# Later heads' scores as three fp32r products in the two halves of TensorE's rows, with three smaller edits to buffers and banks

## The chip, the cores and the metric

The kernel runs on one core of a Trainium2 chip. The core has TensorE (PE, with its weight loads shown apart as PEld), VectorE (DVE), ScalarE (ACT), GpSimd (POOL) and SyncE (SP), which here only issues DMAs. The metric is the device time of one execution in microseconds (us), lower is better. The kernel before takes 1144.28 us, the median of three runs (1142.51 to 1145.09).

## The reference, cut to what matters

Three pieces follow one another, all in fp32. The attention of 4 batches and 8 heads with 576 positions of 64 numbers keeps only the scores within tau of the row's largest; its output, 2304 tokens of 512 numbers, goes through an MLP with 2048 hidden numbers, and that one's through a second with two gates of 1536.

```python
scores = scale * np.matmul(q, k.transpose(0, 1, 3, 2))
thresh = np.max(scores, axis=-1, keepdims=True) - tau
scores = np.where(scores >= thresh, scores, -1000000000.0)
attn = np.exp(scores - np.max(scores, axis=-1, keepdims=True))
x = np.matmul(attn / (np.sum(attn, axis=-1, keepdims=True) + 1e-09), v)   # then heads side by side
h = x @ w_in;  x = (h * (1.0 / (1.0 + np.exp(-h)))) @ w_out               # MLP 1
out = ((x @ w_a) * (x @ w_b)) @ w_o2                                      # MLP 2
```

## The kernel before, in words

**Precision.** An fp32 matrix product is made of products of fp32r numbers: each operand is split into a high part (a cast to fp32r) and a low part (the rest, again fp32r), and high times high, low times high and high times low are summed in PSUM. Scores of the early heads, the transposes of the weighted scores (L577) and the products with v (L622) are plain fp32.

**Order.** All work is a list of tasks with an engine, a rank, an estimated cost and dependences. A planner (`Plan`) plays them through: each engine takes the ready task with the lowest rank. What comes out is a fixed order on each engine, and on the chip every engine works its list in that order. Ring sizes (`RINGS`) say how many buffers of a kind there are; a task that takes one waits for the one that many uses ago. A changed cost or ring can so reorder everything.

**Stages.** (1) Up to about 196 us: attention of batch 0 and part of batch 1, with scores in plain fp32 (L519), and beside it the 32 pieces of MLP 1's weights, loaded and split (`split_weight`). A 64-bit word of a weight is put together from two halves by ScalarE, VectorE (L354, L359) and an integer addition on GpSimd (`total`, L363, four pieces of 128 columns), then split (L367, L371). (2) 196 to 505 us: attention's later heads, with scores in fp32r (L512), mixed on TensorE with MLP 1's products of tokens in blocks of 256 (up L747, down L807). MLP 1's work has a higher rank and fills what attention leaves. (3) 505 to 718 us: MLP 1's last three blocks, of 256, 512 and 512 tokens, and the splitting of MLP 2's weights (`split_unit`), which are written to DRAM again. (4) From 718 us: MLP 2, three times 768 tokens, with seven products in place of eight; up products L1120, down products L1206.

**Scores.** A tile is 128 queries of one head by 576 keys. The keys stand in two halves of 288 (`NH`), one PSUM bank each, index j. For early heads (L519) q stands twice, in SBUF's partitions 0 to 63 and 64 to 127, and k's two halves stand one below the other, so that j = 0 uses the upper 64 rows of TensorE and j = 1 the lower 64. For later heads (from tile 54 on, `SPLIT_FROM`) the operand's 128 partitions hold q's high part above and q's low part below; k's high part stands twice, k's low part twice. One matmul over all 128 rows so gives high times k plus low times k. With k's high and low part and two halves that is four matmuls of 288 columns. Every fifth tile of a pair of heads has 64 queries of one head and 64 of the other: eight matmuls (four of them with 64 columns of weights).

**Closing attention.** Some buffers and PSUM banks of attention are given to MLP 1's last blocks when all of attention's tasks are done (`closed`), the stores of its output among them: the bank hc, the banks yc to yf, the buffers b5 of the 512-token blocks and those (`u`) in which MLP 2's weights are split.

**MLP 2's down products.** Each operand z is split by ScalarE (zh, L971) and VectorE (zl, L975) just before its 12 matmuls; there are two buffers of each. tm holds the sums between products, five buffers.

Of the kernel before, what the change touches and what calls it, by code (L numbers as in the profile page):

```python
# [21 lines left out]
P = 128  # L22
# [198 lines left out]
def pe_ns(n):  # L221
    return int(n * 0.4375 + 7)
# [3 lines left out]
def fused_kernel(ctx: ExitStack, tc: tile.TileContext, qk, qk2, v, tau, w_in, w_out, w_a, w_b, w_o2, out):  # L226
# [21 lines left out]
    def pool(stack, name, bufs, side="left", **kw):  # L248
# [3 lines left out]
    pools = {n: pool(ctx, n, size) for n, size in (("wy", N_YW), ("ws", N_SW), ("wz", N_TW))}  # L252
    p1, p1x, px, att, psb = (ExitStack() for _ in range(5))
    RINGS = dict(qk=2, sp=2, v=1, t=2, e=4, pa=1, pb=1, sa=1, sb=1, tp=2, hb=1, hc=1, yc=1, yd=1, ye=1, yf=1, xr5=2, x5=5, g5=2, th5=1, av=1, x=1, xi=1, rs=1,
                 xr=2, xb=8, g=2, th=1, yo=2, wraw=2, wc=1, wt=2, wy=N_YW, ws=N_SW, wz=N_TW,
                 ur=2, us=2, uw=2, vr=2, vs=2, vw=1, yr=1, pr=4, tm=5, a11=2, zh=2, zl=2, **{f"z{k}": 3 for k in range(5)})

# [17 lines left out]
    x_p = pool(att, "x", RINGS["x"])  # L275
    ps_s = pool(att, "ps_s", 1, space=PSUM)
    ps_t = pool(att, "ps_t", 2, space=PSUM)
    ps_av = pool(att, "ps_av", 1, space=PSUM)

# [48 lines left out]

    def split_weight(key, src, rank, dst, after=(), lo_engine="Pool", scale_engine="DVE", most=512):

# [64 lines left out]
    def w1_chunk(i, rank):  # L395
        dst = w_pool(i)
        j, i = divmod(i, 8)
        engines = dict(scale_engine=SCALE_ON[i % len(SCALE_ON)], lo_engine=LO_ON[i % len(LO_ON)], most=PIECE)
# [15 lines left out]
    def load_head(n, b, h, halves):  # L414
        s = {"split": False}
        cols = slice((0, 256)[halves[0]], (256 + NH, NH + S)[halves[-1]])

        def load():
            s["t"] = ap["qk"].tile([P, 2 * S], F32, name="qk")
            nc.sync.dma_start(out=s["t"][:, cols], in_=qk[b, h, :, cols])  # L420

        ld = dma(n + R_LD, P * 4 * (cols.stop - cols.start), load, take=["qk"])
        att_tasks.append(ld)
        s["ready"] = [ld]
        return s


    def split_head(n, b, h):
        s = {"split": True}

        def load():
            s["r"] = ap["qk"].tile([P, 2 * S], F32, name="qk")
# [6 lines left out]
        def lo_k():  # L439
            nc.vector.tensor_tensor(out=s["t"][:, 2], in0=s["r"][:, S:], in1=s["t"][:, 1].bitcast(F32), op=ALU.subtract)  # L440

        def lo_q(o):
            nc.gpsimd.tensor_tensor(out=s["t"][D:, 0, o], in0=s["r"][D:, o], in1=s["t"][D:, 0, o].bitcast(F32), op=ALU.subtract)

        ld = dma(n + R_LD, P * 8 * S, load, take=["qk"])
        up = add("ACT", act_ns(2 * S), n + R_SPLIT, hi, [ld], ["sp"], behind=closed0)
        qs = on_pool(S, n + R_SPLIT, lo_q, [up], PIECE)
        k = add("DVE", dve_ns(S), n + R_SPLIT, lo_k, [up], port=True)
# [45 lines left out]
    def softmax(parts, total):  # L494
# [203 lines left out]
    def load_x(j):  # L698
# [6 lines left out]
        def split(c):  # L705
# [11 lines left out]

            def lo(o):
                nc.gpsimd.tensor_tensor(out=s["l", c][:, o], in0=s["r", c][:, o], in1=s["h", c][:, o].bitcast(F32), op=ALU.subtract)  # L719
# [3 lines left out]
            l = on_pool(tn, R_AUX, lo, [h], PIECE)[-1]  # L723
            pl.free(raw, l)
# [5 lines left out]
    def mlp1_up(n, j, f):  # L730
# [54 lines left out]
    def mlp1_down(n, j, f):  # L785
# [27 lines left out]
        for k0 in (0, 4, 8):  # L813
            p = pl.add("PE", 4 * pe_ns(tn), R, down(k0), [g_ready[j, f][k0 == 8], *w_ready["out", f]],
                       banks if f == 0 and k0 == 0 else [], behind=[down_last[0], *([closed] if j >= 4 and f == 0 else [])])
            down_last[0] = p
# [446 lines left out]
    closed = pl.add("none", 1, 0, close_attention, behind=[*att_tasks, *closed0])  # L1263
    units = [(j, f) for j in range(len(BLOCKS)) for f in range(NF)]
# [83 lines left out]
```

## Time and profile before

| | before |
|---|---|
| median of 3 runs | 1144.28 us |
| the profiled execution's own time | 1144.45 us |
| its span | 1142.6 us |
| mean granted TensorE clock | 0.987 |
| PE busy | 1105.2 us (97%) |
| DVE busy | 822.8 us (72%) |
| ACT busy | 574.1 us (50%) |
| POOL busy | 201.9 us (18%) |
| chain that ended last | PE 81%, DMA 7%, DVE 5%, ACT 4% |

The span is what the trace covers; the execution's own time is 1.85 us more. Busy times of PE count a matmul from its start to the modelled end of its pipeline, so that neighbours overlap; the distance from one start to the next says more than the length of one. A plain fp32 matmul appears as two records. L with a number is a line of the kernel before.

### The profile page before, as it was taken

The numbers are of one execution on the slowest core, as the hardware profiler recorded it, in microseconds if no ns is written. First come the engines' busy times: TensorE is split into PE (matmuls) and PEld (weight loads), VectorE is DVE, ScalarE is ACT, GpSimd is POOL, SyncE is SP. The second block draws the span as 40 slices with busy tenths as digits, with TensorE's granted clock in tenths as the row PEclk, the third lists the DMA queues.
The fourth block names the chain that finished last, engine by engine and source line by source line (L and its number), as shares of the span: only waits on it lengthen the run. The fifth ranks groups of instructions, "written<-read, shape, count | busy, mean of one in ns | idle before, by whom it ended". The sixth has DMA issues, their size and how long they took to land.

```text
span 1142.6 us, 19524 instructions
## 1 busy us (share of the span) xinstructions
PE 1105.2 (97%) x7097; PEld 985.2 (86%) x7097; DVE 822.8 (72%) x1702; ACT 574.1 (50%) x1012; POOL 201.9 (18%) x386
## 2 busy tenths in 40 slices
PE   8889998999999999999999899999989999999998
PEld 6457766898889989999888688899989999999998
DVE  8888887777777777739888789566764668546664
ACT  7777776666766676646665645311332113411133
POOL 2445444333423343122000200000000000000000
PEclk9989999999999999999999899999999999999999
DMA  6554454222332232139999979988879878887882
GB/s 198 184 166 155 147 156 122 97 80 87 89 98 75 76 104 75 38 123 273 287 269 284 276 219 327 323 247 255 256 261 304 249 255 246 269 281 253 248 252 75
DMA packets 147231, 222.27 MB, mean 195 GB/s; under 512 B 8112, under 2 KB 107584, under 8 KB 147136
## 3 DMA queue, kind: packets, MB, share of 16 engines
q1 hardware_dynamic: 146992, 221.03, 62.4%
q8 instruction: 56, 0.92, 0.3%
q14 instruction: 39, 0.32, 0.1%
q10 hardware_dynamic: 144, 0.00, 0.0%
HBM read 173.74 MB, written 47.26 MB: 193 GB/s over the span
## 4 chain that ended last, share of the span: by engine, by line
PE 81%; DMA 7%; DVE 5%; ACT 4%; issue 2%; POOL 1%; SPq 0%; POOLq 0%; DVEq 0%; ACTq 0%
PE pr L1120 23%; PE hb L747 11%; PE pr L1206 9%; PE sb L807 8%; PE av L622 6%; PE tp L577 5%; PE hc L747 5%; PE sa L512 4%; PE yc L807 2%; PE yd L807 2%; PE ye L807 2%; PE yf L807 2%; DMA wraw<-w_out 1%; DMA xi<-r_d 1%; DMA wraw<-w_in 1%
## 5 line engine op out<-in xcount | busy, mean ns | idle before, releaser
L1120 PE MATMUL pr<-w 128*128 128x384 f32 x1512 | 262.6, 334 | 0.0
L1120 PEld LDWEIGHTS pr<-w 128*128 128x128 f32 x1512 | 262.2, 188 | 0.1
L747 PE MATMUL hb<-xh,w 128*128 128x256 f32 (+1 forms) x704 | 156.9, 312 | 2.6 <-DVE th L760 1.9
L528 DVE TENSOR_SCALAR_CACHE_REDUCE t<-sa,nscale 128x576 f32<-128x576 f32 x128 | 103.5, 809 | 53.0 <-PE sa L512 45.5
L1206 PE MATMUL pr<-zh,w 128*128 128x384 f32 x504 | 129.2, 338 | 0.0
L545 DVE SCALAR_TENSOR_TENSOR e<-t,thr,e 128x576 f32<-128x576 f32 x128 | 112.0, 876 | 23.8 <-ACT e L542 22.3
L747 PEld LDWEIGHTS hb<-xh,w 128*128 128x128 f32 x704 | 113.9, 191 | 12.8 <-DVE th L760 3.1
L577 PE MATMUL tp<-ident,e 128*128 128x128 f32 x706 | 107.5, 280 | 12.0 <-DVE e L545 7.5
L577 PEld LDWEIGHTS tp<-ident,e 128*128 128x128 f32 x706 | 79.7, 142 | 36.4 <-issue 14.2
L542 ACT ACTIVATE e<-t,min 128x576 f32<-128x576 f32 x128 | 99.8, 781 | 19.7 <-DVE t L528 18.7
L747 PE MATMUL hb<-xl,w 128*128 128x256 f32 (+1 forms) x352 | 107.1, 304 | 0.7 <-POOL xl L719 0.7
L807 PE MATMUL sb<-gh,w 128*128 128x256 f32 (+1 forms) x576 | 98.1, 301 | 0.0
L1206 PEld LDWEIGHTS pr<-zh,w 128*128 128x128 f32 x504 | 91.9, 190 | 0.0
L1206 PE MATMUL pr<-zl,w 128*128 128x384 f32 x252 | 86.4, 343 | 4.9 <-DVE zl L975 4.8
L807 PEld LDWEIGHTS sb<-gh,w 128*128 128x128 f32 x576 | 80.1, 190 | 6.3 <-issue 3.3
L971 ACT CAST zh<-z 128x768 fp32r<-128x768 f32 x45 | 37.5, 833 | 84.1 <-PE pr L1206 58.4
L363 POOL TENSOR_TENSOR wt<-wc,wt 128x128 uint32<-128x128 uint32 x128 | 62.3, 517 | 77.3 <-DVE wc L359 48.4
L1132 ACT COPY yo<-pr 128x384 f32<-128x384 f32 x18 | 8.7, 481 | 123.7 <-PE pr L1120 123.7
L747 PEld LDWEIGHTS hb<-xl,w 128*128 128x128 f32 x352 | 67.1, 191 | 3.7 <-POOL xl L719 0.9
L512 PE MATMUL sa<-sp 128*128 128x288 f32 (+1 forms) x400 | 69.9, 300 | 0.0
L584 ACT COPY pb<-tp 128x512 f32<-128x512 f32 (+2 forms) x128 | 60.3, 493 | 17.7 <-PE tp L577 17.5
L719 POOL TENSOR_TENSOR xl<-xr,xh 128x128 fp32r<-128x128 f32 x72 | 39.3, 574 | 165.5 <-ACT xh L716 160.9
(140 smaller groups left out, 2016.6 us busy)
## 6 DMA issues: line engine op xcount, KB each, us to landing
w<-wab_d SPq DMA_DIRECT2D x126, 512.0 KB
w<-wo_d SPq DMA_DIRECT2D x63, 512.0 KB
wab_d<-uw SPq DMA_DIRECT2D x18, 896.0 KB
qk<-qk SPq DMA_DIRECT2D x20, 576.0 KB
wo_d<-uw SPq DMA_DIRECT2D x10, 896.0 KB
wraw<-w_in SPq DMA_DIRECT2D x16, 512.0 KB
wraw<-w_out SPq DMA_DIRECT2D x16, 512.0 KB
v<-v SPq DMA_DIRECT2D x20, 320.0 KB
```

What stands on the lines that cost most here:

```text
L363: nc.gpsimd.tensor_tensor(out=s["t"][:, o], in0=s["c"][:, o].bitcast(U32), in1=s["t"][:, o], op=ALU.add)
L512: nc.tensor.matmul(s["s"][:r + m, j, :NH], lhsT=hd["t"][:, 0, c - r:c + m], rhs=hd["t"][:, k, j * NH:(j + 1) * NH], start=(k == 1), stop=( ...
L528: nc.vector.tensor_scalar(out=s["t"], in0=s["s"][:, :, :NH], scalar1=nscale, scalar2=None, op0=ALU.mult, op1=ALU.min, accum_out=s["min"])
L542: nc.scalar.activation(out=s["e"], in_=s["t"], func=AF.Exp, scale=-1.0, bias=s["min"])
L545: nc.vector.scalar_tensor_tensor(out=s["e"], in0=s["s"][:, :, :NH] if early else s["t"], scalar=s["thr"], in1=s["e"], op0=ALU.is_ge if ear ...
L577: nc.tensor.transpose(t["tp"][:, j * P:(j + 1) * P], e["e"][:, o:o + P], ident)
L584: nc.scalar.copy(out=dst(s["p"]), in_=t["tp"][:, :m * P] if m < 4 else t["tp"].rearrange("p (k q) -> p k q", k=4))
L622: nc.tensor.matmul(s["av"][h * D:(h + 1) * D, :nq], lhsT=v["v"][:, h, k], rhs=s["p"][:, k, h * nq:(h + 1) * nq], start=(k == 0), stop=(k = ...
L747: nc.tensor.matmul(s["h"], lhsT=w[:, a, o:o + P], rhs=xx, start=(c == 0 and k == 0), stop=(c == NC - 1 and k == 2))
L807: nc.tensor.matmul(ys[j][e // per][:, e % per * tn:(e % per + 1) * tn], lhsT=w[:, a, e * P:(e + 1) * P], rhs=gs[j, f][g], start=(f == 0 an ...
L1120: nc.tensor.matmul(bank[:, m, :TN], lhsT=w["w"][:, a, (2 * m + k) * P:(2 * m + k + 1) * P], rhs=y[i][x][:, k, :TN], start=(i in (1, 6, 5) ...
L1206: nc.tensor.matmul(bank[:, c, :TN], lhsT=w["w"][:, a, (2 * e + c) * P:(2 * e + c + 1) * P], rhs=z[x][:, e], start=(i in (1, 6, 5) and sl = ...
```

## The change

- Later heads: q's and k's high parts stand in one operand, the low parts in another, both laid out as for early heads. Three products (high high, low high, high low) are made for each half of the keys, j = 0 in rows 0 to 63 and j = 1 in rows 64 to 127: six matmuls of 288 columns and 64 rows in place of four of 128 rows. What is loaded and split is 864 columns in place of 1152. The planner's cost of a tile is three matmuls in place of four.
- zh has three buffers in place of two, tm four in place of five.
- Attention's PSUM pools stand in a stack of their own, closed when attention's tasks on PE, ACT and DVE are done (`closed_p`). Only hc and the yc to yf banks wait for that; the buffers wait for `closed` as before.
- The integer addition of the weights' third and fourth quarter (j above 1) moves from GpSimd to VectorE, and so does the low part of the last token block's x.
- The planner's costs for MLP 2's weight preparation are lower.

```diff
-                 ..., tm=5, a11=2, zh=2, zl=2, ...
+                 ..., tm=4, a11=2, zh=3, zl=2, ...
...
-    ps_s = pool(att, "ps_s", 1, space=PSUM)
+    ps_s = pool(attp, "ps_s", 1, space=PSUM)
...
         def total(o):
-            nc.gpsimd.tensor_tensor(out=s["t"][:, o], in0=s["c"][:, o].bitcast(U32), in1=s["t"][:, o], op=ALU.add)
+            eng = nc.gpsimd if total_engine == "Pool" else nc.vector
+            eng.tensor_tensor(out=s["t"][:, o], in0=s["c"][:, o].bitcast(U32), in1=s["t"][:, o], op=ALU.add)
...
+        ..., total_engine=("Pool", "DVE")[j > 1])
...
         def hi():
-            s["t"] = pools["sp"].tile([P, 3, S], F32R, name="sp")
-            nc.scalar.copy(out=s["t"][:, :2], in_=s["r"].rearrange("p (a s) -> p a s", a=2))
+            s["t"] = pools["sp"].tile([P, 2, S + NH], F32R, name="sp")
+            nc.scalar.copy(out=s["t"][:, 0], in_=s["r"])
...
+        def lo(eng, o):
+            eng.tensor_tensor(out=s["t"][:, 1, o], in0=s["r"][:, o], in1=s["t"][:, 0, o].bitcast(F32), op=ALU.subtract)
...
                 for hd, c, r, m in reversed(parts):
-                    for j in range(2):
-                        for k in (1, 2):
-                            nc.tensor.matmul(s["s"][:r + m, j, :NH], lhsT=hd["t"][:, 0, c - r:c + m], rhs=hd["t"][:, k, j * NH:(j + 1) * NH],
-                                             start=(k == 1), stop=(k == 2), skip_group_check=True)
+                    for k, (a, x) in enumerate(((0, 0), (1, 0), (0, 1))):
+                        for j in range(2):
+                            rows = slice(j * D, (j + 1) * D)
+                            nc.tensor.matmul(s["s"][:r + m, j, :NH], lhsT=hd["t"][rows, a, c - r:c + m], rhs=hd["t"][rows, x, S:],
+                                             start=(k == 0), stop=(k == 2), skip_group_check=True)
...
-        cost = 4 * pe_ns(NH) * len(parts) if parts[0][0]["split"] else 780
+        cost = 3 * pe_ns(NH) * len(parts) if parts[0][0]["split"] else 780
...
+            if j == len(BLOCKS) - 1:
+                l = pl.add("DVE", dve_ns(tn), R_AUX, lambda: lo(slice(0, tn), nc.vector), [h], port=True)
...
-                       behind=[up_last[0], *([closed] if c == 0 and bank == "hc" else [])])
+                       behind=[up_last[0], *([closed_p] if c == 0 and bank == "hc" else [])])
...
+    def close_banks():
+        attp.close()
         pools["hc"] = pool(p1, "ps_hc", 1, space=PSUM)
         pools["y5"] = pool(p1, "ps_y5", 1, space=PSUM)
...
+    closed_p = pl.add("none", 1, 0, close_banks, behind=[t for t in att_tasks if t["engine"] in ("PE", "ACT", "DVE")])
```

What it moves, at three places. First, TensorE at the first mixed tile of the later heads; L512 and L514 are the scores, L577 and L579 transposes, L622 and L624 products with v, L747, L752, L807 and L812 MLP 1. Before:

```order
L577 MATMUL tp<-ident,e 128x128 x6
L512 MATMUL sa<-sp 128x288 x4
L627 MATMUL av<-ident,sums 128x128
L807 MATMUL sb<-gh,w 128x256 x4
L807 MATMUL sb<-gl,w 128x256 x4
L622 MATMUL av<-pa,v 64x256 x10
L577 MATMUL tp<-ident,e 128x128 x4
L512 MATMUL sa<-sp 128x288 x4
L512 MATMUL sa<-sp 64x288 x4
L577 MATMUL tp<-ident,e 128x128 x6
```

And of the changed kernel, at its first mixed tile:

```order
L812 MATMUL sb<-gh,w 128x256 x4
L514 MATMUL sa<-sp 128x288 x6
L812 MATMUL sb<-gh,w 128x256 x4
L579 MATMUL tp<-ident,e 128x128 x6
L812 MATMUL sb<-gl,w 128x256 x4
L629 MATMUL av<-ident,sums 128x128
L624 MATMUL av<-pa,v 64x256 x10
L579 MATMUL tp<-ident,e 128x128 x4
L514 MATMUL sa<-sp 128x288 x6
L514 MATMUL sa<-sp 64x288 x6
L579 MATMUL tp<-ident,e 128x128 x6
```

A tile's scores stand alone between other matmuls, as before: there are 90 such places in either order, and no two tiles' scores follow one another.

Second, ScalarE where the 512-token block before the last ends: yo copies the sums out of PSUM (L827, L832), th and gh belong to the next block's first units, us, vs, uw and vw to MLP 2's weights. Before:

```order
L827 ACTIVATE yo<-ye 128x512
L827 ACTIVATE yo<-sb 128x512
L898 CAST vw<-vs 128x896
L757 ACTIVATE th_8561<-hb 128x512
L870 ACTIVATE vs<-vr 128x512
L873 ACTIVATE vs<-vr 128x512
L763 CAST gh_8562<-th_8561 128x512
```

And of the changed kernel:

```order
L832 ACTIVATE yo<-ye 128x512
L875 ACTIVATE us<-ur 128x512
L878 ACTIVATE us<-ur 128x512
L762 ACTIVATE th_8730<-hb 128x512
L903 CAST vw<-vs 128x896
L768 CAST gh_8731<-th_8730 128x512
L832 ACTIVATE yo<-sb 128x512
```

The copy out of sb stood ahead of the next block's th and gh and now stands behind them; a pair us that needs a loaded weight stands ahead of th.

Third, SyncE in MLP 2's first down products: w are the streamed weights, yr the next 768 tokens' input. Before:

```order
L960 DMA w<-wab_d 128x1024 x30
L960 DMA w<-wo_d 128x1024 x15
L995 DMA yr<-yT_d 128x2x768
L960 DMA w<-wo_d 128x1024
L995 DMA yr<-yT_d 128x2x768
L960 DMA w<-wo_d 128x1024 x5
```

And of the changed kernel:

```order
L965 DMA w<-wab_d 128x1024 x30
L965 DMA w<-wo_d 128x1024 x13
L1000 DMA yr<-yT_d 128x2x768
L965 DMA w<-wo_d 128x1024 x2
L1000 DMA yr<-yT_d 128x2x768
L965 DMA w<-wo_d 128x1024 x6
```

The two loads of yr are issued two and one weight loads earlier.

## Rows read from the trace of the kernel before

**Rows 1.** The page's first line.
```profile
span 1142.6 us, 19524 instructions
```

**Rows 2.** Four stretches: busy of PE, PEld, DVE, ACT, POOL; granted clock, DMA share, GB/s.
```profile
0.00:196.00 196.00, 173.92 (x1193) 122.96 (x1193) 159.48 (x417) 145.70 (x279) 83.34 (x173) 0.96 0.53 161
196.00:505.00 309.00, 307.93 (x2491) 276.43 (x2491) 223.03 (x623) 201.02 (x391) 101.51 (x186) 1.00 0.27 83
505.00:718.00 213.00, 208.05 (x1071) 177.23 (x1070) 180.89 (x349) 129.13 (x213) 17.06 (x29) 0.98 0.92 276
718.00:1142.00 424.00, 415.27 (x2347) 408.54 (x2345) 259.40 (x315) 98.23 (x130) 0.00 (x0) 0.99 0.79 250
```

**Rows 3.** Later heads' scores by form: count, busy us, mean ns, idle before.
```profile
L512 PE MATMUL sa<-sp 128*128 128x288 f32 x360 | 64.6, 301 | 0.0
...
L512 PE MATMUL sa<-sp 128*64 128x288 f32 x40 | 6.9, 294 | 0.0
```

**Rows 4.** PE in time, one later tile: start, length, instruction.
```profile
301.31 0.69 PE L512 MATMUL sa<-sp 128*128 128x288 f32 x4
...
301.84 0.64 PE L807 MATMUL sb<-gl,w 128*128 128x256 f32 x4
```

**Rows 5.** PE and PEld in time, an early tile between MLP 1's matmuls.
```profile
104.07 0.64 PE L807 MATMUL sb<-gh,w 128*128 128x256 f32 x4
104.64 0.76 PE L519 MATMUL sa<-qk 64*128 64x288 f32 x4
105.32 0.74 PE L807 MATMUL sb<-gh,w 128*128 128x256 f32 x4
105.90 0.28 PE L807 MATMUL sb<-gl,w 128*128 128x256 f32 x1
...
105.32 0.54 PEld L807 LDWEIGHTS sb<-gh,w 128*128 128x128 f32 x4 [0.39 <-issue]
```

**Rows 6.** PE in time, the first two tiles, right behind plain fp32 matmuls.
```profile
4.29 0.50 PE L287 MATMUL av<-sums 128*128 128x128 f32 x3
4.72 0.76 PE L519 MATMUL sa<-qk 64*128 64x288 f32 x4
5.31 0.65 PE L519 MATMUL sb<-qk 64*128 64x288 f32 x4
5.89 0.33 PE L575 MATMUL tp<-ident 128*128 128x128 f32 x1
```

**Rows 7.** PE in time, a later mixed tile, its last four with 64 columns.
```profile
309.96 1.29 PE L512 MATMUL sa<-sp 128*128 128x288 f32 x8
311.09 0.27 PE L577 MATMUL tp<-ident,e 128*128 128x128 f32 x1
```

**Rows 8.** ACT and PE in time where the next-to-last block of MLP 1 ends.
```profile
646.30 0.60 ACT L827 ACTIVATE yo<-sb 128x512 f32<-128x512 f32 x1 [3.17 <-DMA yT_d<-yo]
...
647.63 0.60 ACT L757 ACTIVATE th<-hb 128x512 f32<-128x512 f32 x1
...
651.00 1.22 PE L807 MATMUL yc<-gh,w 128*128 128x512 f32 x2 [4.30 <-ACT gh L763]
```

**Rows 9.** Two stretches, columns as in Rows 2.
```profile
640.00:660.00 20.00, 15.70 (x58) 12.33 (x57) 14.80 (x30) 10.91 (x18) 2.03 (x4) 0.83 0.96 289
840.00:860.00 20.00, 17.53 (x94) 17.21 (x93) 12.00 (x13) 5.89 (x8) 0.00 (x0) 0.91 0.74 251
```

**Rows 10.** PE and DVE in time, down products of MLP 2.
```profile
833.20 0.44 PE L1206 MATMUL pr<-zl,w 128*128 128x384 f32 x1 [0.78 <-DVE zl L975]
...
841.39 0.96 DVE L1007 TENSOR_TENSOR yt<-yr 128x768 f32<-128x768 f32 x1 [2.25 <-DMA yr<-yT_d]
...
844.27 0.69 PE L1206 MATMUL pr<-zl,w 128*128 128x384 f32 x1 [2.47 <-DVE zl L975]
```

**Rows 11.** Groups: the integer addition on DVE (MLP 2's) and POOL.
```profile
L887 DVE CUSTOM_DVE_ANT_0 us<-us 128x1024 uint16<-128x1024 uint16 x28 | 19.2, 684 | 0.0
...
L363 POOL TENSOR_TENSOR wt<-wc,wt 128x128 uint32<-128x128 uint32 x128 | 62.3, 517 | 77.3 <-DVE wc L359 48.4 <-DVE thr L536 18.5 <-DVE sums L477 5.9
```

More of the change, by code (lines that the diff above doesn't have):

```diff
@@ L252, in fused_kernel @@
     pools = {n: pool(ctx, n, size) for n, size in (("wy", N_YW), ("ws", N_SW), ("wz", N_TW))}
-    p1, p1x, px, att, psb = (ExitStack() for _ in range(5))
+    p1, p1x, px, att, attp, psb = (ExitStack() for _ in range(6))
     RINGS = dict(qk=2, sp=2, v=1, t=2, e=4, pa=1, pb=1, sa=1, sb=1, tp=2, hb=1, hc=1, yc=1, yd=1, ye=1, yf=1, xr5=2, x5=5, g5=2, th5=1, av=1, x=1, xi=1, rs=1,
                  xr=2, xb=8, g=2, th=1, yo=2, wraw=2, wc=1, wt=2, wy=N_YW, ws=N_SW, wz=N_TW,
-                 ur=2, us=2, uw=2, vr=2, vs=2, vw=1, yr=1, pr=4, tm=5, a11=2, zh=2, zl=2, **{f"z{k}": 3 for k in range(5)})
+                 ur=2, us=2, uw=2, vr=2, vs=2, vw=1, yr=1, pr=4, tm=4, a11=2, zh=3, zl=2, **{f"z{k}": 3 for k in range(5)})
     right = ctx.enter_context(ExitStack())
@@ L275, in fused_kernel @@
     x_p = pool(att, "x", RINGS["x"])
-    ps_s = pool(att, "ps_s", 1, space=PSUM)
-    ps_t = pool(att, "ps_t", 2, space=PSUM)
-    ps_av = pool(att, "ps_av", 1, space=PSUM)
+    ps_s = pool(attp, "ps_s", 1, space=PSUM)
+    ps_t = pool(attp, "ps_t", 2, space=PSUM)
+    ps_av = pool(attp, "ps_av", 1, space=PSUM)
     sums = const.tile([P, P], F32, name="sums")
@@ L327, in fused_kernel, with split_weight @@
     wt, w_ready = {}, {}
-    def split_weight(key, src, rank, dst, after=(), lo_engine="Pool", scale_engine="DVE", most=512):
+    def split_weight(key, src, rank, dst, after=(), lo_engine="Pool", scale_engine="DVE", most=512, total_engine="Pool"):
         s = {}
@@ L379, in split_weight @@
         j = pl.add("DVE", dve_ns(512), rank, join, [h, c], port=True)
-        ts = on_pool(512, rank, total, [j, l], most)
+        if total_engine == "Pool":
+            ts = on_pool(512, rank, total, [j, l], most)
+        else:
+            ts = [pl.add("DVE", dve_ns(512), rank, lambda: total(slice(0, 512)), [j, l], port=True)]
         pl.free("wc", ts[-1])
@@ L397, in w1_chunk @@
         j, i = divmod(i, 8)
-        engines = dict(scale_engine=SCALE_ON[i % len(SCALE_ON)], lo_engine=LO_ON[i % len(LO_ON)], most=PIECE)
+        engines = dict(scale_engine=SCALE_ON[i % len(SCALE_ON)], lo_engine=LO_ON[i % len(LO_ON)], most=PIECE, total_engine=("Pool", "DVE")[j > 1])
         if i < 4:
@@ L418, in load @@
         def load():
-            s["t"] = ap["qk"].tile([P, 2 * S], F32, name="qk")
+            s["t"] = ap["qk"].tile([P, S + NH], F32, name="qk")
             nc.sync.dma_start(out=s["t"][:, cols], in_=qk[b, h, :, cols])
@@ L431, in load @@
         def load():
-            s["r"] = ap["qk"].tile([P, 2 * S], F32, name="qk")
+            s["r"] = ap["qk"].tile([P, S + NH], F32, name="qk")
             nc.sync.dma_start(out=s["r"], in_=qk2[b, h])
         def hi():
-            s["t"] = pools["sp"].tile([P, 3, S], F32R, name="sp")
-            nc.scalar.copy(out=s["t"][:, :2], in_=s["r"].rearrange("p (a s) -> p a s", a=2))
[L439 to L448, printed above, removed]
+            s["t"] = pools["sp"].tile([P, 2, S + NH], F32R, name="sp")
+            nc.scalar.copy(out=s["t"][:, 0], in_=s["r"])
+        def lo(eng, o):
+            eng.tensor_tensor(out=s["t"][:, 1, o], in0=s["r"][:, o], in1=s["t"][:, 0, o].bitcast(F32), op=ALU.subtract)
+        ld = dma(n + R_LD, P * 4 * (S + NH), load, take=["qk"])
+        up = add("ACT", act_ns(S + NH), n + R_SPLIT, hi, [ld], ["sp"], behind=closed0)
+        qs = on_pool(S, n + R_SPLIT, lambda o: lo(nc.gpsimd, o), [up], PIECE)
+        k = add("DVE", dve_ns(NH), n + R_SPLIT, lambda: lo(nc.vector, slice(S, S + NH)), [up], port=True)
         att_tasks.extend([ld, *qs])
@@ L716, in hi, with lo @@
                 nc.scalar.copy(out=s["h", c], in_=s["r", c])
-            def lo(o):
-                nc.gpsimd.tensor_tensor(out=s["l", c][:, o], in0=s["r", c][:, o], in1=s["h", c][:, o].bitcast(F32), op=ALU.subtract)
+            def lo(o, eng=nc.gpsimd):
+                eng.tensor_tensor(out=s["l", c][:, o], in0=s["r", c][:, o], in1=s["h", c][:, o].bitcast(F32), op=ALU.subtract)
             ld = dma(-1, P * 4 * tn, load, after=need, take=[raw], slack=SLACK, behind=[closed] if big else [])
             h = pl.add("ACT", act_ns(tn), R_AUX, hi, [ld], [ring])
-            l = on_pool(tn, R_AUX, lo, [h], PIECE)[-1]
+            if j == len(BLOCKS) - 1:
+                l = pl.add("DVE", dve_ns(tn), R_AUX, lambda: lo(slice(0, tn), nc.vector), [h], port=True)
+            else:
+                l = on_pool(tn, R_AUX, lo, [h], PIECE)[-1]
             pl.free(raw, l)
@@ L814, in mlp1_down @@
             p = pl.add("PE", 4 * pe_ns(tn), R, down(k0), [g_ready[j, f][k0 == 8], *w_ready["out", f]],
-                       banks if f == 0 and k0 == 0 else [], behind=[down_last[0], *([closed] if j >= 4 and f == 0 else [])])
+                       banks if f == 0 and k0 == 0 else [], behind=[down_last[0], *([closed_p] if j >= 4 and f == 0 else [])])
             down_last[0] = p
@@ L849, in dv @@
     def dv(n):
-        return int(n / 0.96 + 170)
+        return int(n / 0.96 + 67)
     def ac(n):
-        return int(n / 1.2 + 180)
+        return int(n / 1.2 + 93)
     stored = {}
```

5 lines of the change are left out of this document (2 added, 3 removed).

## The prediction

> **What bounds the kernel now.** I read the span [rows 1], then the table of busy times by stage [rows 2]. From 196 to 505 us, where the later heads' scores stand, PE is busy 307.93 of 309 us at full clock; VectorE 223, ScalarE 201, and DMA's share is 0.27. The reader is to see that whatever TensorE gains or loses there is gained or lost by the whole, and that edits on other engines in that stage (a shorter cast, a shorter VectorE subtraction, a smaller load) are worth nothing. Before 196 us PE lacks 22 us and VectorE is busy 159 of 196: neither is full. From 505 to 718 and from 718 on PE is full again but for a few single waits, found by reading PE's timeline for gaps [rows 8, 10].
>
> **The scores.** Before: 360 + 40 matmuls [rows 3], four to a part, so 100 parts, of which ten pairs make mixed tiles: 90 separate places on PE. One tile of four takes 301.84 - 301.31 = 0.53 us, 0.13 us a matmul [rows 4], and loses nothing at its ends. Together 400 x 0.13 = 52 us.
>
> After: 600 matmuls over half the rows. Whether two of them run side by side, the early heads show: their matmuls use 64 rows in the same alternation. And they show what it costs to go into the halves and out again. In [rows 5] four matmuls of MLP 1 take 0.64 us to the last's end and one alone 0.28, so they start 0.12 us apart. From 104.07 to 105.90 us there are eight of them, 0.96 us; the tile between takes 1.83 - 0.96 = 0.87 us. How much of this is streaming? Two tiles on end take 5.89 - 4.72 = 1.17 us to the next instruction [rows 6], one takes 105.32 - 104.64 = 0.68 [rows 5]: the second tile costs 0.49 us. It has four records of 288 columns. Plain fp32 over all rows takes 0.11 us for one of 128 columns (three in 0.50 us less the 0.27 of one alone [rows 6, 7], halved), so 0.25 for 288, and four in a row 1.0 us: the halves do run side by side. The remaining 0.87 - 0.49 = 0.38 us are lost at the two changes: TensorE starts 104.64 - 104.07 - 4 x 0.12 = 0.09 us late, then waits for its first weights; behind the tile the next weight load starts only after 0.39 us without one, in which nothing is named as awaited [rows 5], where otherwise weights are loaded under the matmul before.
>
> Is that the halves' doing or plain fp32's? In [rows 6] plain fp32 matmuls over all 128 rows stand ahead of the first tile: three from 4.29 us on, at 0.11 us, should let the next start at 4.62 and it starts at 4.72. The number type doesn't change there, the rows do. Against this stands [rows 7]: 128 columns of weights to 64, in fp32r, costs nothing (eight in 1.13 us). So a change of columns alone is free in fp32r; a change of rows in fp32r no row shows. I take the 0.38 us for each place.
>
> The Trainium skill has rules for both sides. Its page "TensorEngine Tiling (Array Packing)", section Key Properties, says that a change of the tiling mode drains the engine; that agrees with [rows 5, 6] and speaks against this change, though [rows 7] shows a change of columns without one; it states no price, so the sum goes by the rows. "TensorE: Matmul & The Clock Gate", Part 3, lets tiles in different rows run at the same time, some 4 ns apart, and by that alone the change would save a quarter of the scores' time; [rows 6] agrees with the concurrency.
>
> After, then: 100 parts x 3 x 0.13 = 39 us, 13 less than before; 90 x 0.38 = 34 us more; within a mixed tile a change from 128 to 64 columns of weights in halved rows, ten times 0 [rows 7] to 0.38 us, I take 1 us. **Sum +22 us.** Its ends: -13 (nothing lost at the changes) and, with halves one after another, 600 x 0.13 - 52 + 34 = +60.
>
> **The third zh.** PE waits for zl 0.78 us at 833 us, as long again at the same place of the next 768 tokens, and 2.47 us at 844 [rows 10]. The first two are the cast that waits for one of two zh; with three, two casts stand ahead of the copy of the sums. The long one is VectorE, which sits 2.25 us at L1007 until yr has landed, with the zl behind it; yr's loads now stand one and two weight loads earlier, and a product of 12 matmuls (each such load feeds one) lasts about 2 us, so it should land in time. The clock was 0.91 from 840 to 860 us [rows 9]: 20 x 0.09 x 2 = 3.6 us at 1.2 GHz instead of 2.4, in part the wait itself, so about 1 us lost. Together 0.78 + 0.78 + 2.47 + 1 = **-5 us**; ends 0 and -6. The missing fifth tm would show as PE waiting for a copy behind the output's stores; no wait of this kind is near, I give it 0.
>
> **The last-but-one block's end.** PE waits 4.30 us for gh; ScalarE stood 3.17 us before the copy of sb, waiting for a store of yo to land, and th and gh were queued behind it [rows 8]. The clock is 0.83 there [rows 9], 6.8 us at the lower level, about 2 us lost beyond the wait. In the new order th and gh go first, but a pair us, which needs a loaded weight while DMA's share is 0.92 [rows 2], stands ahead of them. **-4 us**; ends -6.5 and +3 (the same wait at another place).
>
> **The first stage.** Sixteen integer additions go to VectorE: the same operation for MLP 2's weights takes 0.684 us [rows 11], 16 x 0.684 = 11 us on an engine with 36 us free; 64 pieces of 0.517 us leave GpSimd. A weight's chain gets shorter by 4 x 0.517 - 0.684 = 1.4 us, the weights are split before tile 45 instead of 54 in VectorE's order, and 474 instead of 408 matmuls of MLP 1 stand ahead of the first later score, 66 x 0.12 = 8 us of work for PE's 22 idle us. So +11 to -8; I take **0**.
>
> **Banks, and the later close.** The order leaves 66 instead of 159 matmuls of MLP 1 between the last score and the first use of hc: attention ends 11 us nearer to it. The banks' own wait is covered by 66 x 0.12 = 8 us. What still waits for `closed` starts that much later against PE: the 512-token blocks' loads, covered by the 256-token block's 16 units of 24 matmuls, 46 us; and MLP 2's weights, where DMA's share is 0.92 [rows 2] and SyncE's and ScalarE's queues are held up with it. I take 0; if that cover is gone it costs up to 11 us. The last block's x on VectorE: 0, four operations where it has 32 us free.
>
> **Sum.** 22 - 5 - 4 = +13. The profiled execution took 1144.45 us (span 1142.6 and 1.85 around it), 0.2 above the median of the runs. 1144.45 + 13 = **1158 us**.
>
> **Rivals.**
> - *The change of rows is free in fp32r*, as that of columns is [rows 7]. Then the scores save 13 us, and with the other gains 1144.45 - 13 - 9 = 1122: faster than before. For it: no row shows fp32r in halves; against it: [rows 6]. It decides where a place costs below (13 + 9) / 90 = 0.24 us; there the change is even. By the Trainium skill's Part 3 named above this would be the outcome.
> - *Half the price*: the wait for the rows to empty, but weights loaded ahead. 90 x 0.19 = 17: +17 - 13 - 9, about 1140.
> - *fp32r halves take turns*, though fp32's don't, so that the change doesn't do what it says: 600 x 0.13 = 78 us, 1158 + 39 = 1197.
>
> **How the numbers follow.** The forecast has 0.74, its own range 1146 to 1172 (-12: first stage and ends of the waits' terms; +14: late weights or waits that stay). Free rows 0.16, half the price 0.05, turns 0.05. 0.2% of the time, 2.3 us, is about what can be told from no change. Faster: 0.16 + 0.03 + 0.01 of the forecast's tail = 0.20. Same 0.05. Slower 0.75. To leave out no more than 2 in 10 the range reaches into the free rows' case: 1120 to 1173.
>
> **What would show it.** PE's timeline around the new scores: a tile of six should take about 0.8 us between its neighbours' rhythm, with a stretch without weight loads behind it; at 0.4 us the first rival is right, at 1.2 or more the last. The two halves should start within 0.01 us. MLP 1's 256-token block should start some 20 us later than 505. At the down products the waits for zl should be gone, as should the 4.3 us for gh. If PE in the stage of the later heads shows waits for other engines, the bound was read wrongly.

## The result, and the profile after

The changed kernel takes 1151.56 us (median of 5 runs, 1148.4 to 1154.17) against 1143.87 of the kernel before (1140.46 to 1145.09): ratio 1.0068, 95% interval 1.0042 to 1.0094. It is slower, by 7.7 us where 13 were forecast. The profiled execution's span grew from 1142.6 to 1149.8 us.

The same four stretches as in [rows 2], of the changed kernel (busy of PE, PEld, DVE, ACT, POOL; granted clock, DMA share, GB/s):

```profile
0.00:196.00 196.00, 176.06 (x1238) 127.60 (x1238) 168.03 (x436) 145.49 (x282) 54.23 (x113) 0.97 0.51 161
196.00:505.00 309.00, 308.93 (x2553) 251.62 (x2552) 212.40 (x609) 191.34 (x376) 85.78 (x174) 1.00 0.22 68
505.00:718.00 213.00, 204.66 (x1085) 171.83 (x1085) 176.72 (x355) 128.98 (x219) 11.82 (x20) 0.98 0.90 270
718.00:1142.00 424.00, 423.90 (x2398) 417.49 (x2397) 263.06 (x323) 102.39 (x136) 0.00 (x0) 1.00 0.80 257
```

The reader is to see three things. In the second stretch PE is as full as before. In the third PE's busy time fell from 208.05 to 204.66 us: there something is waited for that was not waited for before. In the fourth it rose from 415.27 to 423.90 us: waits are gone.

By landmarks on PE (start of the first later score; of the first matmul into hc, which opens the 256-token block; of MLP 2's first product; the span's end):

| us | first later score | first hc | MLP 2 begins | end | hc to MLP 2 | MLP 2 |
|---|---|---|---|---|---|---|
| before | 207.4 | 505.8 | 735.9 | 1142.6 | 230.1 | 406.8 |
| after | 205.2 | 516.2 | 752.0 | 1149.8 | 235.8 | 397.8 |

So +10.4 up to hc, +5.7 up to MLP 2, -9.0 in MLP 2.

A later tile in the changed kernel, PE in time, to be read beside [rows 4, 5], the weight load behind it, and one ahead of the products with v a little later:

```profile
204.77 0.40 PE L752 MATMUL hb<-xh,w 128*128 128x256 f32 x2
205.01 0.28 PE L752 MATMUL hb<-xl,w 128*128 128x256 f32 x1
205.22 0.66 PE L514 MATMUL sa<-sp 64*128 64x288 f32 x6
205.81 0.50 PE L752 MATMUL hb<-xh,w 128*128 128x256 f32 x2
206.16 0.28 PE L752 MATMUL hb<-xl,w 128*128 128x256 f32 x1
...
205.81 0.30 PEld L752 LDWEIGHTS hb<-xh,w 128*128 128x128 f32 x2 [0.16 <-issue]
...
210.32 1.81 PEld L624 LDWEIGHTS av<-pb,v 128*64 128x64 f32 x16 [0.16 <-issue]
```

From 205.01 to 205.81 are 0.80 us, of which 0.12 belong to the single matmul; the two matmuls behind the tile take 0.35 us to the next start where two ahead of it take 0.24. The tile of six costs 0.80 - 0.12 + 0.35 - 0.24 = 0.79 us. Before, a tile of four cost 0.53. Added up over all 90 places by the distances of starts, the scores cost 53.9 us before and 74.4 after: **+20.5 us**, forecast +22. The first records of the two halves start 3 to 4 ns apart, so they run side by side.

PE's waits between 505 and 752 us of the changed kernel (engine, line, what for: us in total, times, longest):

```profile
PE yc L812 <- ACT gh L768: 3.3, 3, 2.1
PE hb L752 <- ACT xh L718: 2.4, 1, 2.4
PE hb L752 <- DVE xl L721: 1.4, 1, 1.4
PE ye L812 <- ACT gh L768: 1.1, 3, 0.6
```

The one wait of 4.30 us [rows 8] is gone, and smaller ones at other places, 8.2 us together, have come for it. PE and ACT in time around the longest wait for gh:

```profile
689.80 0.74 PE L812 MATMUL yc<-gh,w 128*128 128x512 f32 x2 [2.13 <-ACT gh L768]
...
685.36 0.67 ACT L875 ACTIVATE us<-ur 128x512 uint32<-128x512 uint32 x1 [2.69 <-DMA ur<-w_o]
...
686.77 0.59 ACT L762 ACTIVATE th<-hb 128x512 f32<-128x512 f32 x1
...
689.15 0.60 ACT L768 CAST gh<-th 128x512 fp32r<-128x512 f32 x1
```

ScalarE stands 2.69 us for a weight of MLP 2 that has not landed, and th and gh are queued behind it, with four more operations on these weights among them. In MLP 2 of the changed kernel no wait of PE is left; before there were seven for zl, of which [rows 10] shows two:

```profile
PE pr L1206 <- DVE zl L975: 4.8, 7, 2.5
```

### The profile page after: what moved, and what is told of

Read it like the earlier page. It is cut to its first block, busy times and chain, and to the rows that moved or that the text cites. A ratio compares the mean times of both kernels' runs of the same rounds, so it can differ in the third digit from the quotient of the medians.

```text
span 1149.8 us, 19765 instructions
## 1 busy us (share of the span) xinstructions
PE 1116.9 (97%) x7286; PEld 971.6 (85%) x7286; DVE 821.4 (71%) x1722; ACT 568.2 (49%) x1012; POOL 151.8 (13%) x306
## 4 chain that ended last, share of the span: by engine, by line
PE 70%; DMA 11%; DVE 9%; ACT 4%; issue 3%; POOL 2%; SPq 1%; ACTq 0%; POOLq 0%; DVEq 0%
PE pr L1125 23%; PE pr L1211 11%; PE hb L752 8%; PE sb L812 6%; PE tp L579 5%; PE sa L514 5%; PE av L624 5%; PE hc L752 2%; DMA xi<-r_d 2%; DMA xT_d<-x 1%; DMA wraw<-w_in 1%; PE yc L812 1%; DMA wraw<-w_out 1%; PE yd L812 1%; POOL wt L364 1%
## 5 line engine op out<-in xcount | busy, mean ns | idle before, releaser
L752 PE MATMUL hb<-xh,w 128*128 128x256 f32 (+1 forms) x704 | 159.7, 317 | 3.6 <-ACT xh L718 2.4
L547 DVE SCALAR_TENSOR_TENSOR e<-t,thr,e 128x576 f32<-128x576 f32 x128 | 109.1, 853 | 26.2 <-ACT e L544 25.1
L752 PEld LDWEIGHTS hb<-xh,w 128*128 128x128 f32 x704 | 112.1, 190 | 18.4 <-issue 6.7
L579 PE MATMUL tp<-ident,e 128*128 128x128 f32 x706 | 109.1, 282 | 11.2 <-DVE e L547 9.4
L579 PEld LDWEIGHTS tp<-ident,e 128*128 128x128 f32 x706 | 79.0, 142 | 37.6 <-issue 19.3
L752 PE MATMUL hb<-xl,w 128*128 128x256 f32 (+1 forms) x352 | 106.7, 303 | 1.9 <-DVE xl L721 1.4
L812 PE MATMUL sb<-gh,w 128*128 128x256 f32 (+1 forms) x576 | 97.9, 302 | 0.0
L812 PEld LDWEIGHTS sb<-gh,w 128*128 128x128 f32 x576 | 79.0, 189 | 9.7 <-issue 6.0
L752 PEld LDWEIGHTS hb<-xl,w 128*128 128x128 f32 x352 | 66.7, 189 | 5.0 <-DVE xl L721 1.8
L768 ACT CAST gh<-th 128x256 fp32r<-128x256 f32 (+1 forms) x112 | 52.2, 466 | 36.2 <-DVE th L765 35.7
L771 DVE TENSOR_TENSOR gl<-th,gh 128x256 fp32r<-128x256 f32 (+1 forms) x112 | 58.8, 525 | 13.1 <-ACT gh L768 12.8
L659 POOL TENSOR_TENSOR x<-x,xi 128x128 f32<-128x128 f32 (+2 forms) x80 | 43.3, 565 | 183.8 <-DMA xi<-r_d 105.1
```

Source lines behind the costliest of these rows:

```text
L547: nc.vector.scalar_tensor_tensor(out=s["e"], in0=s["s"][:, :, :NH] if early else s["t"], scalar=s["thr"], in1=s["e"], op0=ALU.is_ge if ear ...
L579: nc.tensor.transpose(t["tp"][:, j * P:(j + 1) * P], e["e"][:, o:o + P], ident)
L752: nc.tensor.matmul(s["h"], lhsT=w[:, a, o:o + P], rhs=xx, start=(c == 0 and k == 0), stop=(c == NC - 1 and k == 2))
L771: nc.vector.tensor_sub(out=s["gl"], in0=s["t"], in1=s["gh"].bitcast(F32))
L812: nc.tensor.matmul(ys[j][e // per][:, e % per * tn:(e % per + 1) * tn], lhsT=w[:, a, e * P:(e + 1) * P], rhs=gs[j, f][g], start=(f == 0 an ...
```

## The experiments

Ratios are to the kernel before, run on the same chip in the same session; five rounds each unless said. The kernel before had medians from 1139.89 to 1143.87 us in these sessions, so two experiments are compared by their ratios. Times of stretches are of one profiled execution each. Line numbers differ a little from kernel to kernel.

### The price of changing rows, by itself

The kernel before with test matmuls at its start and four buffers of tm, run once: always four fp32r matmuls of 256 columns over all rows (L296), and between them what is tested, six times over: (a) one matmul of 288 columns over all rows, (b) one in each half of the rows, (c) three such pairs, (d) one half alone, (e) two on end in one half, (f) 64 columns of weights over all rows, (g) plain fp32, 128 x 128, over all rows. The code of (b):

```diff
+    def half(j, o=slice(0, P)):
+        r = slice(j * D, (j + 1) * D)
+        nc.tensor.matmul(pad[o, j, :NH], lhsT=ones[r, :o.stop - o.start], rhs=ones[r], start=True, stop=True)
...
+    for _ in range(6):
+        full()
+        half(0)
+        half(1)
...
```

> The kernel before (tm = 4) with a row of test matmuls ahead of its first task, all fp32r unless said, four full ones of 256 columns between any two: (a) one more full one of 288, (b) one pair in the two halves of the rows, (c) three pairs, (d) one matmul in the upper half, (e) two on end in the upper half, (f) 64 columns of weights over all rows, (g) one plain fp32 matmul of 128 columns over all rows. The time of the whole says nothing; what counts is the distance between starts. Theory (a change of rows empties the array and keeps the next weights from being loaded ahead): (a) 0.13 us, (b) 0.52, (c) 0.78, (d) 0.52 as the pair, (e) 0.65, (f) 0.13, (g) about 0.11 for each of its passes. Rival (the price comes with two tiles at once, or with plain fp32): (d) near 0.13, or (g) 0.4 above its two passes.

PE in time, two neighbouring starts of each test:

```profile
8.19 0.30 PE L308 MATMUL sa<-ones 128*128 128x288 f32 x1
8.32 0.64 PE L296 MATMUL av<-ones 128*128 128x256 f32 x4
8.79 0.30 PE L308 MATMUL sa<-ones 128*128 128x288 f32 x1
...
11.91 0.40 PE L300 MATMUL sa<-ones 64*128 64x288 f32 x2
12.24 0.74 PE L296 MATMUL av<-ones 128*128 128x256 f32 x4
12.91 0.40 PE L300 MATMUL sa<-ones 64*128 64x288 f32 x2
...
17.90 0.67 PE L300 MATMUL sa<-ones 64*128 64x288 f32 x6
...
19.16 0.67 PE L300 MATMUL sa<-ones 64*128 64x288 f32 x6
...
25.47 0.39 PE L300 MATMUL sa<-ones 64*128 64x288 f32 x1
...
26.47 0.39 PE L300 MATMUL sa<-ones 64*128 64x288 f32 x1
...
31.41 0.53 PE L300 MATMUL sa<-ones 64*128 64x288 f32 x2
...
32.53 0.53 PE L300 MATMUL sa<-ones 64*128 64x288 f32 x2
...
38.08 0.29 PE L303 MATMUL sa<-ones 128*64 128x288 f32 x1
...
38.68 0.29 PE L303 MATMUL sa<-ones 128*64 128x288 f32 x1
...
41.68 0.39 PE L330 MATMUL sa<-sums 128*128 128x128 f32 x2
...
42.38 0.38 PE L330 MATMUL sa<-sums 128*128 128x128 f32 x2
```

The four over all rows take 8.79 - 8.32 = 0.47 us; the rest of a period is the test. (a) 0.60 - 0.47 = 0.13, (b) 1.00 - 0.47 = 0.53, (c) 1.26 - 0.47 = 0.79, (d) 0.53, (e) 0.65, (f) 0.13, (g) 0.70 - 0.47 = 0.23 for two records. What loses time is the change of rows alone: a single half (d) costs as much as a pair (b), while 64 columns (f) and another number type (g) cost only their streaming. The rival falls. Take the 0.13 us of one pass from 0.53 and 0.40 us are left, against 0.38 in the prediction.

### The scores taken back, and the scores alone

The changed kernel with the later heads' scores, their operands and their cost as before:

```diff
-                    for k, (a, x) in enumerate(((0, 0), (1, 0), (0, 1))):
+                    for j in range(2):
+                        for k in (1, 2):        # four matmuls over all rows
```

> The changed kernel with the later heads' scores as they were (four fp32r products over all 128 rows, 1152 columns loaded and split), all its other edits kept. Theory: the halved rows cost 90 x 0.39 = 35 us of changes and save 13 us of streaming, so taking them out gives back about 22 us: 1151.6 - 22 = about 1130, some 14 us faster than before; stages other than the later heads' as in the changed kernel, MLP 2 about 398 us from its first matmul to the end. Rival (the new order on the engines, not the rows, is what costs, and the 0.39 us were largely covered): between 1145 and 1152, since the order's other parts stay.

Measured: 1134.2 us, ratio 0.9935 (0.9909 to 0.9961), against 1.0068 of the changed kernel: 1.3% given back, some 15 us.

The kernel before with the scores' part of the change and nothing else:

> The kernel before with the scores' edit alone. Theory: +21 to +23 us, 1165 to 1167, all of it between the first later score and MLP 1's last blocks; MLP 2 stays at about 407 us. Rival (rows cost little, the rest of the edits brought the loss): 1144 to 1152.

Measured: 1157.72 us, ratio 1.0151 (1.0126 to 1.0176). Its 90 places cost 74.4 us. The first falls near the theory's 1130. The second, 1.5% or 17 us, lies between the two ranges, nearer the theory's. Both are less than the 20.5 us at the tiles.

### One product instead of three

The changed kernel, run once, the two products with low parts left out:

```diff
-                    for k, (a, x) in enumerate(((0, 0), (1, 0), (0, 1))):
+                    for k, (a, x) in enumerate(((0, 0),)):
```

> The changed kernel with only the high x high product of each later part: one pair of matmuls, one in each half of the rows, where there were three pairs; the two products with low parts are left out. Theory (0.39 us for each place where the rows change, halves side by side): a tile of one pair keeps the whole price and loses two pairs of 0.13 us, so about 0.52 us at 80 places, and a mixed tile about 0.65 at ten, 48 us in all against the 74 of the changed kernel. Rival (the six matmuls of a tile take turns, 6 x 0.13 = 0.78 us, and a change costs nothing): 0.26 us a tile and 0.52 a mixed one, 26 us in all.

Its 90 places cost 47.6 us (0.52 a tile of one pair, 0.61 a mixed one): the theory's 48. With a third of the matmuls the scores still cost nearly what four full matmuls a part cost. But from the first later score to hc the time fell from 311.0 us to 290.0, by 21.0 and not by the 26.8 saved at the tiles. PE's longest waits from 206 to 495 us of this kernel:

```profile
PE tp L579 <- ACT pb L586: 4.0, 3, 2.5
PE sb L812 <- DVE yo L834: 0.4, 1, 0.4
```

In the changed kernel there is none in that stretch. So the stage has little room under PE: made cheaper, it begins to wait for ScalarE. That is one part of why taking the scores back gave less than 20.5 us (there PE's waits in that stretch come to 3.3 us).

### The third zh alone

```diff
-    ..., tm=5, a11=2, zh=2, ...
+    ..., tm=4, a11=2, zh=3, ...
```

> The kernel before with zh = 3 and tm = 4 alone. Theory: MLP 2 goes from 407 to about 398 us as in the changed kernel, so 1144 - 9 = 1135. Rival (the buffers gave the two waits of 0.78 us, and the wait for yr at 841 us went because yr's loads came to stand earlier for other reasons): -2 to -4, 1140 to 1142.

Measured: 1134.64 us, ratio 0.9940 (0.9917 to 0.9963), some 7 us; MLP 2 took 400.1 us instead of 406.8, and PE's waits for zl fell from 4.8 to 1.1 us. That is nearer the theory than the rival.

### The additions, from both sides

The experiment before this one with sixteen of MLP 1's integer additions on VectorE:

```diff
+        ..., total_engine=("Pool", "DVE")[j > 1])
```

> The kernel before with the third zh and, beside it, sixteen integer additions of MLP 1's later weights on VectorE instead of GpSimd; scores, banks and the last block's x as before. It differs from the third experiment (1134.6 us) by the additions alone. Theory (the additions are worth nothing): 1131 to 1138 us. Rival (they are worth 8 us in the first stage): 1125 to 1129 us, and about 470 matmuls of MLP 1 ahead of the first later score.

And the kernel with the scores taken back, with the additions on GpSimd again:

> The changed kernel with the later heads' scores as before, and with the integer additions for MLP 1's later weights on GpSimd as before too. It differs from the first of these experiments (1134.2 us) by the additions alone. Theory (the additions are worth nothing, since the first stage is bound by no single engine): 1131 to 1138 us. Rival (the shorter chain of a weight gave the first stage its 8 to 10 us): 1140 to 1145 us, and fewer matmuls of MLP 1 ahead of the first later score, 408 instead of 484.

Measured: 1128.07 us, ratio 0.9894 (0.9871 to 0.9918), and 1137.42 us, ratio 0.9980 (0.9966 to 0.9993). By their times the first lies in the rival's range and the second in the theory's. By the ratios (0.9894 against 0.9940, 0.9980 against 0.9935) the additions on VectorE are worth 0.45% from either side, 5 us, so the theory of "nothing" falls. But the place is not the rival's first stage: first hc stands at 500.7 us with the additions moved and at 499.9 without. Hc to MLP 2 is 224.5 against 229.3 us, and in the other pair 231.8 against 235.3. The new order happens to leave ScalarE's casts more nearly in time there: PE's waits for gh at yc fell from 5.1 us to 0.8 in the first pair.

### The planner told the price of a tile

```diff
-        cost = 3 * pe_ns(NH) * len(parts) ...
+        cost = 390 + 3 * pe_ns(NH) * len(parts) ...
```

> The changed kernel, with the planner told 390 ns more for each later score tile, so that it lays out the order by the cost that the trace shows. Theory (the price is the chip's, at each place, and the order adds little): the 90 places cost 74 us as before, and the time stays within 1147 to 1156 us. Rival (the planner's too low cost put attention's end too near to the 512-token blocks, which is what the stage from 516 to 752 us lost): 4 to 8 us come back, 1143 to 1147 us, and that stage takes 230 instead of 236 us.

Measured: 1152.37 us, ratio 1.0108 (1.0088 to 1.0129). The places cost 73.7 us, hc to MLP 2 took 238.0: the theory's outcome, nothing came back. MLP 2's first weights reached ScalarE 9 us ahead of hc here, and that stage was still slow: their lateness alone was not its cause.

### The planner's costs for MLP 2's weights

To the experiment with zh and the additions, the change's lower costs, which alter the order only from the 512-token blocks on:

```diff
-        return int(n / 0.96 + 170)      # dv;  ac: n / 1.2 + 180
+        return int(n / 0.96 + 67)       #      ac: n / 1.2 + 93
-        h = pl.add("DVE", 600, rank, sign, ...)
+        h = pl.add("DVE", 335, rank, sign, ...)
```

> The experiment with the third zh and the additions on VectorE (1128.1 us), and beside it the planner's lower costs for MLP 2's weight operations (dv and ac 103 and 87 ns less, the sign 335 instead of 600). The order changes only from the 512-token blocks of MLP 1 on. Theory (the lower costs let us<-ur, which waits for DMA, stand ahead of xh and gh on ScalarE): from the first hc to MLP 2's first matmul 229 to 232 us instead of 224.5, and 1131 to 1136 us. Rival (that loss comes from the banks closed apart or from the last block's x on VectorE): 224 to 226 us there, and 1125 to 1130 us.

Measured: 1141.72 us, ratio 0.9992 (0.9977 to 1.0007); hc to MLP 2 243.6 us instead of 224.5. The direction is the theory's, the size far above it: the costs alone lose 1% here. The stretch from 560 to 700 us with the old costs, then with the lower ones (columns as in the four stretches above):

```profile
560.00:700.00 140.00, 139.16 (x601) 112.89 (x600) 119.96 (x229) 83.31 (x128) 7.58 (x12) 1.00 0.94 278
```

```profile
560.00:700.00 140.00, 128.34 (x534) 102.50 (x533) 126.53 (x239) 86.53 (x135) 8.57 (x12) 0.96 0.97 290
```

The lower costs draw MLP 2's weights together. From 580 to 680 us DMA's share is 1.02 to 1.05 with them and 0.84 to 0.99 without, and ScalarE, which stands for weights that have not landed, lets PE wait for gh: 6.8 and 5.7 us at yc and ye.

The low parts of the last block's x on VectorE, added to the same experiment:

```diff
+                l = pl.add("DVE", dve_ns(tn), R_AUX, lambda: lo(slice(0, tn), nc.vector), [h], port=True)
```

> The same experiment (1128.1 us), and beside it the last block's low parts of x on VectorE; costs and banks as before. Theory (the planner's costs are what lost the time at the 512-token blocks): from the first hc to MLP 2's first matmul 224 to 226 us, and 1125 to 1131 us. Rival (x on VectorE makes them late, as PE's wait of 1.4 us for xl shows): 228 to 231 us there, and 1131 to 1135 us.

Measured: 1127.07 us, ratio 0.9861 (0.9836 to 0.9885), hc to MLP 2 225.5: this edit costs nothing, and the kernel has the lowest ratio of all that ran, though its interval overlaps that of the kernel without the edit (0.9871 to 0.9918).

The changed kernel with those costs as before:

> The changed kernel with the planner's costs for MLP 2's weight operations as before, all else changed. The order differs only from the 512-token blocks on. Theory (the costs lost the time there): from the first hc to MLP 2's first matmul 225 to 231 us instead of 235.8, the scores still 74 us, and 1142 to 1148 us. Rival (attention's end, 11 us nearer to these blocks, lost it): 234 to 238 us there, and 1149 to 1155 us.

Measured: 1151.39 us, ratio 1.0070 (1.0050 to 1.0089). The stage is quick, 221.8 us, even below the theory's bound, but the time is the rival's: nothing is won. (In this order twelve matmuls of MLP 1, 2.75 us, stand behind MLP 2's first twelve and so count for MLP 2.) MLP 2 takes 413.3 instead of 397.8 us. PE at its beginning, VectorE, and the stretch around them:

```profile
760.04 15.21 PE L1125 MATMUL pr<-w 128*128 128x384 f32 x70 [6.38 <-DVE tm L1061]
...
756.30 0.96 DVE L1012 TENSOR_TENSOR yt<-yr 128x768 f32<-128x768 f32 x1 [7.15 <-DMA yr<-yT_d]
```

```profile
740.00:760.00 20.00, 12.29 (x66) 11.15 (x64) 10.17 (x17) 4.18 (x6) 0.00 (x0) 0.90 1.04 344
760.00:780.00 20.00, 19.96 (x99) 19.96 (x100) 9.21 (x13) 1.28 (x2) 0.00 (x0) 0.85 0.68 214
```

VectorE stands 7.15 us for yr, with the sum that PE needs queued behind it. DMA is full up to 760 us, and behind the wait PE runs at a mean granted clock of 0.85, so part of these 20 us at 1.2 GHz instead of 2.4. Counted against PE's rhythm (each matmul at the usual distance of its shape from the next), MLP 2 lost 13.6 us.

### Weights that start later

Is that backlog in DMA the late start of MLP 2's weights, which the prediction had bounded by 11 us? In the changed kernel the first cast of such a weight begins at 527.48 us, 11.3 behind hc; before at 505.55, 0.3 ahead of it. The experiment with zh and the additions, where it is 3.0 us behind hc, with banks closed apart and attention's buffers held by one small VectorE copy that the planner puts some 9 us later:

```diff
+    idle = pl.add("none", 9000, 0, lambda: None, behind=[*att_tasks, *closed0, closed_p])
+    hold = pl.add("DVE", 67, 0, lambda: nc.vector.tensor_copy(out=held, in_=late), [idle])
-    closed = pl.add("none", 1, 0, close_attention, behind=[*att_tasks, *closed0])
+    closed = pl.add("none", 1, 0, close_attention, behind=[*att_tasks, *closed0, hold])
```

> The experiment with the third zh and the additions on VectorE (1128.1 us), banks closed apart, old planner costs, scores as before, and attention's buffers held by one VectorE copy that stands some 9 us later, so that MLP 2's first weights are loaded about as much later against the first hc as in the changed kernel (their first cast 11 us behind hc instead of 3). Theory (late weights cost the changed kernel about 10 us, at the 512-token blocks or at MLP 2's start, whichever way the planner orders them): from the first hc to the end 632 to 637 us instead of 625, and 1134 to 1141 us. Rival (the weights' start is covered, and only the planner's costs lose time): 623 to 628 us from hc, and 1125 to 1131 us.

Measured: 1134.83 us, ratio 0.9929 (0.9903 to 0.9954), against 0.9894 without the delay. The first cast comes 9.1 us behind hc, 6.1 later than without, and from hc to the end it takes 631.0 us instead of 625.2: 5.8 more, a little under the theory's 632. The sign is that of the last experiment, PE and VectorE at MLP 2's start:

```profile
741.78 18.48 PE L1128 MATMUL pr<-w 128*128 128x384 f32 x96 [3.23 <-DVE tm L1060]
...
737.16 0.96 DVE L1015 TENSOR_TENSOR yt<-yr 128x768 f32<-128x768 f32 x1 [2.29 <-DMA yr<-yT_d]
```

So with the old planner costs the start of these weights has no cover. How much it costs is less sure than the sign: the 5.8 us compare one execution with one, that of the later start was the longest of its six (1138.9 us), the two ratios differ by 0.35%, 4 us, with intervals that just overlap, and the edit closes the banks apart as well.

## Why the prediction was right, and where not

*The scores: right.* Forecast +22 us, measured +20.5 at the 90 places. The stretch from the first later score to hc, all at full clock, took 316.7 us with the scores alone and 297.5 in the kernel with the third zh alone, whose order is the old one there: +19.2. The number type does not matter: the price read from plain fp32 tiles [rows 5, 6] was that of the rows, 0.40 us beside 0.38. Halves run side by side, and the change from 128 to 64 columns inside a mixed tile costs nothing (its twelve matmuls cost 1.14 us, less than 0.40 and six pairs of 0.13), where I had taken 1 us in all. The sign behind the tile did not hold: weights stop for 0.16 us there, not 0.39, and for as long ahead of the products with v, where only the columns change. The rivals (free rows, half the price, turns) fall with it. The Trainium skill's page "TensorEngine Tiling (Array Packing)", section Key Properties, says that the engine drains when the tiling mode changes: the runs agree for the rows, at 0.40 us, and not for a change of columns alone, which cost nothing in (f).

*"Whatever TensorE gains or loses there is gained or lost by the whole": too strong.* PE busy 307.93 of 309 [rows 2] does not say what stands just below it. With cheaper scores PE waited 3 to 4 us for ScalarE in that stage; a slower PE in turn covers such waits. The scores alone so cost the whole 1.5%, 17 us.

*Up to hc: +10.4 us, where 22 were summed and "some 20 us later than 505" was named as the sign.* The scores did cost that much. But in the profiled execution the kernel before was late for another reason. These are the kernel before, the one with the third zh alone, and the changed kernel, each up to its first later score (columns as in [rows 2]):

```profile
0.00:207.40 207.40, 185.14 (x1275) 132.36 (x1276) 168.25 (x437) 153.81 (x295) 90.73 (x187) 0.96 0.52 158
0.00:202.47 202.47, 181.32 (x1276) 130.60 (x1276) 168.49 (x437) 152.59 (x295) 91.25 (x187) 0.98 0.53 162
0.00:205.22 205.22, 185.21 (x1308) 134.82 (x1309) 173.94 (x452) 152.00 (x295) 58.01 (x120) 0.98 0.50 158
```

The first two have the same order up to hc and take 298.4 and 297.5 us from there to hc, so of the 5.9 us between them at hc (505.8 and 499.9) 4.9 lie in the first stage, where the granted clock was 0.96 and 0.98. Against 499.9 the changed kernel's hc at 516.2 is 16.3 us late. With the scores alone hc is at 520.0, so the other edits bring 3.8 us: 66 more of MLP 1's matmuls stand ahead of the first later score.

*The third zh: right, sized low.* Forecast -5. MLP 2 became 9.0 us shorter, 6.7 with zh alone, since all seven waits for zl went and not three, and with them stretches at a lower clock (0.99 before, 1.00 after).

*The last-but-one block's end: wrong.* Forecast -4, its other end +3; measured +5.7 between hc and MLP 2. The named wait for gh went, but the step looked at one wait and not at what ScalarE's queue waits for; the pair us ahead of th, which it named for the other end, was one of several. The lower planner costs, for which the prediction has no term at all, set weight casts that wait for DMA ahead of xh and gh. On another kernel the same edit cost 1%, and taken back in the changed kernel it made this stage 14 us shorter, of which 2.75 are the landmark's.

*Banks and the later close: the value 0 holds only in part, the bound of 11 us is about right.* With the old planner costs a start later by 6.1 us cost 5.8, and the changed kernel, whose weights come 11.5 us later against hc than before, lost 13.6 us in MLP 2 with them. With its own, lower costs it pays 12.2 us between hc and MLP 2 against PE's rhythm there (372 matmuls at 0.120 us and 768 at 0.233, 223.6 us), but no run puts that down to the late start: the stage was as slow where these weights came 9 us ahead of hc (238.0 us) or 0.5 behind it (235.3, with the scores and the additions as before). The two losses don't add, and why not is open. The 512-token blocks' cover of 46 us was read for their own loads; for the weights the full DMA queue was the thing to read.

*The first stage: 0 was right up to hc with the old scores, and wrong for the time.* With the additions moved 76 more of MLP 1's matmuls, some 9 us of work, stand ahead of the first later score; from there to hc only 3.0 us are won (294.5 against 297.5), and PE now waits 3.6 us there. The additions also shift the order of everything behind them, and with that 5 us at the 512-token blocks.

The time came out 6 us below the forecast: MLP 2 gained 4 us more than its term, the part up to hc lost 10.4 us where 22 were summed for it, and between hc and MLP 2 the 4 us of gain became 5.7 of loss. That the sum still came out near is in part luck: misses of 4 and 11.6 us one way and 9.7 the other partly cancel, and some 5 of the 11.6 are the lower clock in the profiled execution of the kernel before. The sign rests on one term, the scores; without it the same change is 0.65% faster than before, and the third zh with the additions and x on VectorE is 1.4% faster.

## What to carry to other kernels

Count the places at which TensorE goes from all rows to part of them and back, and multiply by the 0.4 us measured here: products in halved rows pay only where many follow one another. When a planner's costs are edited, price the new order at each queue that waits for DMA, since an operation set ahead of another there makes the other wait as well. A full engine tells what a loss costs, not what a gain brings: look for what is nearly as late.

## What the runs showed of the hardware

- Going from 128 rows to 64 and back costs 0.40 us beyond the streaming, between fp32r matmuls of 256 columns, the same for one half, for a pair and for three pairs; going from 128 to 64 columns at the first column (0.13 us a matmul, as with 128), or from fp32r to plain fp32 (0.23 us for two records), costs nothing.
- Within the halves a further pair costs 0.13 us, as one matmul over all rows does; two on end in one half also 0.12 (0.65 - 0.53).
- Behind PE's waits of 1.37 and 6.38 us at MLP 2's start (the changed kernel with the old planner costs) the granted clock was 0.85 over the next 20 us.
